# A list scheduler that reckons with longer transposing DMAs: the same work in another static order

## The chip, the cores and the metric

The kernel runs on one core of one Trainium2 chip. The metric is the device time of one execution in microseconds (us), lower is better; the time before is the median of three executions. The core has a matrix engine (PE, with its weight loads shown apart as PEld), a vector engine (DVE), a scalar engine (ACT), a general engine (POOL) and a queue engine (SP) that issues DMAs. ACT issues some DMAs too. Each engine runs its own list of instructions strictly in the order in which it stands, and semaphores make it wait for the others.

## The reference, cut to what matters

```python
# attention with a threshold: batch 4, heads 8, 576 positions, head size 64
scores = q @ k^T / 8
thresh = max(scores) - tau
scores = where(scores >= thresh, scores, -1e9)
attn   = exp(scores - max) / (sum + 1e-9)
x      = (attn @ v) as 2304 tokens x 512
# dense layer pair, leaky ReLU
h = x @ w_in;  g = max(0.01 * h, h);  x = g @ w_out          # 512 -> 2048 -> 512
# soft mixture of 8 experts, 4 slots each
logits = x @ phi                                              # 2304 x 32
d = softmax of logits over the tokens;  slot_in = d^T @ x
slot_out[e] = relu(slot_in[e] @ w1[e]) @ w2[e]                # 512 -> 1024 -> 512
out = (softmax of logits over the slots) @ slot_out
```

All inputs are float32, and w_in and w_out arrive as 64-bit patterns that the kernel takes apart.

## The kernel before

The 2304 tokens are worked in 18 tiles of 128. For each tile, `attention(t)` makes four pairs of heads. For one pair PE computes the scores of both heads (line 1087, called S here), DVE takes the negated row maximum (line 1100, nm), ACT the exponential (line 1121, ae), DVE the masked product and the row sum (line 1128), ACT rounds the result to half precision (line 1154, the high half of ah) and POOL subtracts to get the low half (line 1164). A transposing DMA on SP then turns each head's ah, nine blocks of 128x128, into aT (line 1186, two a pair, 144 in all), and PE multiplies aT with the values into the tile X (line 1196, called X here, 14 matmuls for a head). After eight heads DVE scales X into x32, PE transposes it (line 1229), and ACT and DVE write it as xT.

`feed(t)` multiplies xT with w_in in four column groups of 12 matmuls (line 1267, called H here, dealt out in portions of three), ACT and POOL or DVE make the two halves of r (lines 1280, 1286, 1289), a transposing DMA of eight blocks makes rT (line 1312, 72 in all), and PE multiplies rT with a product of w_out and phi into the logits of the tile (lines 1322 and 1326, called L here). `block` adds every two tiles to the running softmax over tokens. The last part, the tail, starts when the logits of tile 17 are there: it loads w1 and w2 through loads of 256 KB each on SP (line 1691, 128 of them, besides 16 loads of line 1627) into whatever buffers the main part has given free, multiplies (lines 1660, 1703, 1771) and stores the output.

No order is written by hand. Every piece of work is handed to `Plan.add` with a duration and a priority, and `Plan.schedule` is a list scheduler: it keeps a model of each engine's free time, of buffers and of the DMA engines, picks again and again the piece that can start first (the priority breaks ties), and appends it to that engine's list. Where a piece has alternatives (DVE or POOL, SP's queue or ACT's), it also picks the engine. The result is the static order in which the program is emitted; the durations act at planning time alone. A transposing DMA goes through `dma_t`: its `ns` is the time for which the model's DMA engines are held; SP itself is held by `op.hold`, whose first number is a formula in the blocks and whose second, 1300 ns, is the time from issue to the first transfer. The table `LAT` adds 942 ns between the end of a DMA and the PE instruction that reads its data. So the plan before lets PE read an aT 1300 + 9 x 112 + 942 = 3250 ns after its issue if the DMA engines are free.

Of the kernel before, what the change touches and what calls it, by code (L numbers as in the profile page):

```python
# [341 lines left out]
def emit(tc, a, out, dbg=None, opt=None):  # L342
    nc = tc.nc
    pe, act, dve, pool, sp = nc.tensor, nc.scalar, nc.vector, nc.gpsimd, nc.sync
    ctx = ExitStack()
    pl = Plan()
# [37 lines left out]
    one = lambda e, ns, f: [(e, ns, f)]  # L384
# [13 lines left out]
    def const(shape, dt=F32):  # L398
        uniq[0] += 1
        n = f"c{uniq[0]}"  # L400
        pl.tag(n, "const", 1)
        return pl.buf(n, shape, dt)
# [43 lines left out]

    def dma_t(prio, blocks, fn, r=(), w=(), after=()):

        op = pl.add(prio, one("sp", 112.0 * blocks, fn), r, w, after)
        op.hold = (max(1225.0, 398.0 + 112.0 * blocks), 1300.0)  # L450
        return op

    def dump(name, b, sel, prio=1e9):
# [13 lines left out]
        r=[ident], w=[e4],  # L467
# [4 lines left out]
        r=[e4], w=[e96],  # L472
# [9 lines left out]
        r=[tau], w=[sg],  # L482
# [6 lines left out]
        r=[tau], w=[nt],  # L489
# [235 lines left out]
    for k in range(4):  # L725
# [19 lines left out]
        r=[zf], w=[zfr],  # L745
# [17 lines left out]
    for c in range(FF // P):  # L763
        PQ = PO + O["PS"] * c
        here = c < O["RES"]
        w = one_chunk(
            PQ, a["w_out"], c * P, 0, (O["TO"], O["TU"], "raw_out"),
            dst=const([P, DM]) if here else None,
        )
# [5 lines left out]
                r=[w],  # L775
# [5 lines left out]
        def f(w=w, tp=tp):  # L781
# [11 lines left out]
            r=[tp], w=[wt],  # L793
# [3 lines left out]
        def f(wt=wt, wpp=wpp):  # L797
# [7 lines left out]
            r=[wpp], w=[(wp32, c)],  # L805
# [7 lines left out]
        r=[wp32], w=[pm],  # L813
# [8 lines left out]
        r=[spw], w=[wp32],  # L822
# [9 lines left out]
        r=[wp32, (wq, 0)], w=[(wq, 1)],  # L832
    )
    wlq = const([P, 4, 2 * NS], F16) if O["TR"] < O["TE"] else None
    if wlq:
# [3 lines left out]
        for k in range(4):  # L839
            wts = []  # L840
            for j in range(4):
                wt = tmp([P, 8, P], F16, O["TL"])
                dma_t(
                    PL + 0.01 * k, 8,
                    (lambda k, j, wt: lambda: sp.dma_start_transpose(
                        out=wt.ap, in_=wh[k][j].ap.rearrange("p a b -> p (a b)")))(k, j, wt),
                    r=[wh[k][j], wq], w=[wt],
                )
                wts.append(wt)
            lp = tmp([P, 2 * NS], F32, "misc")  # L850

            def f(wts=wts, lp=lp):
# [16 lines left out]
                r=[lp], w=[(wl32, k)],  # L869
# [7 lines left out]
            w=[wl32],  # L877
# [9 lines left out]
            r=[wl32, (wlq, 0)], w=[(wlq, 1)],  # L887
# [247 lines left out]
    def attention(t):  # L1135
# [5 lines left out]
        for pr in range(4):  # L1141
# [40 lines left out]
            for i in range(2):  # L1182
                aT = pl.buf("aT", [P, 9, P], F16)
                dma_t(
                    p2, 9,
                    (lambda ah, aT, i: lambda: sp.dma_start_transpose(out=aT.ap, in_=ah.ap[:, i]))(ah, aT, i),
                    r=[(ah, (n, i)) for n in range(3)], w=[aT],
                )

                todo = [(c, wv, 4 * i + c) for wv in range(2) for c in range(4)]  # L1190
                todo += [(4, wv, 8 + i) for wv in range(2)] + [(5 + c, 0, 4 * i + c) for c in range(4)]

                def f(pr=pr, i=i, aT=aT, todo=todo):
                    for r0, r1, b in regs:
                        for n, (c, wv, cv) in enumerate(todo):
                            pe.matmul(  # L1196
                                out=X.ap[r0:r1, 2 * pr + i], lhsT=aT.ap[:, c, r0:r1],
                                rhs=vtiles[b, pr].ap[:, wv, cv], start=(pr == 0 and i == 0 and n == 0),
                                stop=(n == len(todo) - 1), skip_group_check=True,
                            )  # L1200

                pe_op(
                    p + 0.22, 29 * 14 * len(regs), f, r=[aT] + [vtiles[b, pr] for b in parts], w=[X],
                )
# [48 lines left out]
    def feed(t, xT, xh):  # L1253
# [4 lines left out]
        for j in range(4):  # L1258
# [37 lines left out]
            else:  # L1296
# [11 lines left out]
                    r=[hp, (r[j], 0)], w=[(r[j], 1)],  # L1308
                )
            dma_t(  # L1310
                p + 0.1, 8,
                (lambda j: lambda: sp.dma_start_transpose(
# [308 lines left out]
    for c in range(FF // P):  # L1621
        if wos[c]:
# [5 lines left out]
            w=[wo], after=[stores[c]], la=2 if c < O["NA"] else 0,  # L1628
# [58 lines left out]
    def load(src, prio, shape=(P, 512)):  # L1687
        w = pl.buf(CH, shape, F32, "ch")
        nld[0] += 1
        la = 2 if 16 + nld[0] <= O["NA"] else 0  # L1690
        lds.append(dma(prio, t_dma(P * 512 * 4), lambda dq: dq.dma_start(out=w.ap, in_=src), w=[w], la=la))
        return w

    for G in range(2):
        for n in range(2):
            h1 = pl.buf("S", [P, 512])
            for k in range(4):
                for j in range(4):
                    e = 4 * G + j
                    w = load(a["w1"][e, k * P : (k + 1) * P, n * 512 : (n + 1) * 512], T0 - 7)  # L1700
# [6 lines left out]
                        r=[sit, w], w=[(h1, j)],  # L1707
# [26 lines left out]
    for t0 in range(0, NTILE, 4):  # L1734
        m = min(4, NTILE - t0)
        e3, cp = tbuf([P, m, 3, NS]), pl.buf("misc", [96, m, P])
        if t0 % 8 == 0:
# [4 lines left out]
            r=[(ecs, t) for t in range(t0, t0 + m)], w=[e3])  # L1742

        def f(m=m, e3=e3, cp=cp):
# [8 lines left out]
            op=ALU.subtract))(cp, ct, o4, m), r=[cp], w=[(ct, o4)])  # L1753
# [5 lines left out]
    for hf in range(2):  # L1759
        pt = T0 + 2 + hf  # L1760
        for G in range(2):
            for c in range(0, 8, 2):
                for j in range(4):
                    q = hts[G]
                    w = load(
                        a["w2"][hf, 4 * G + j, c // 2].rearrange("p (k d) -> p k d", k=2), T0 - 7, [P, 2, HC]
                    )
# [26 lines left out]
        for t in range(0, NTILE, 2):  # L1794
            op, ot = pl.buf(("h", "S", "misc")[t // 2 % 3], [P, 2, HC]), pl.buf(CH, [P, 2, HC], F32, "ot")
# [7 lines left out]
            for i in range(2):  # L1803
# [10 lines left out]
                    r=[op, rc], w=[(ot, i)],  # L1814
# [5 lines left out]
                r=[ot], la=2,  # L1820
# [57 lines left out]
```

## Time and profile before

| what | value |
|---|---|
| median of 3 executions | 628.68 us (627.34 to 630.64) |
| the profiled execution, own time | 625.68 us |
| its span, first to last instruction | 623.9 us |
| mean granted clock of PE | 0.969 |
| busy in the span: PE, DVE, ACT, POOL | 509.2, 438.0, 425.3, 342.9 us |

The span has three parts: about 80 us in which inputs are loaded and w_in is taken apart, about 440 us in which the 18 tiles go through, and the rest, in which the last tile's feed ends and the tail runs. The profiled execution is 3.0 us quicker than the median. "Busy" is the time in which an engine had an instruction running; who waited for whom is inferred from semaphores.

### The profile page before, as it was taken

Reading aid. Unit: us, or ns where it says so; the run is one execution under the profiler, and the core shown is the slowest. Engines: PE = TensorE matmul, PEld = TensorE weight load, DVE = VectorE, ACT = ScalarE, POOL = GpSimd, SP = SyncE. Lnnn points to the kernel's source line nnn. Section 1 sums busy time; section 2 is a strip of 40 time slices with the busy share of each in tenths; the row PEclk is TensorE's granted clock in tenths of the full one; section 3 lists DMA queues with packets and bytes.
Section 4 is the critical chain, followed back from the end, with each engine's and each line's share of the span. In section 5 each row is a group of like instructions: output and inputs, shape, how many; then the busy total and the mean of one; then the engine's idle time right before and its main releaser. Section 6 shows DMA issues by size and latency. Waiting matters only on the chain.

```text
span 623.9 us, 15356 instructions
## 1 busy us (share of the span) xinstructions
PE 509.2 (82%) x5694; PEld 318.3 (51%) x5694; DVE 438.0 (70%) x1055; ACT 425.3 (68%) x802; POOL 342.9 (55%) x381
## 2 busy tenths in 40 slices
PE   0111698998899998898999899998999798479995
PEld 0001586666566665555555556565656454223653
DVE  6999978889779777878879777765878743211133
ACT  7999778987668777878978787777777752212012
POOL 3445444775667565787877767777787650000000
PEclk9999998999999999999999999999999989779997
DMA  8972799998899998999999999999998999999998
GB/s 315 328 270 63 209 229 210 236 231 181 177 226 195 220 194 142 197 158 205 228 191 149 173 166 167 212 203 199 183 174 155 212 190 268 288 392 386 379 394 316
DMA packets 287018, 140.55 MB, mean 225 GB/s; under 512 B 251616, under 2 KB 251616, under 8 KB 286944
## 3 DMA queue, kind: packets, MB, share of 16 engines
q1 hardware_dynamic: 281472, 129.05, 91.2%
q10 hardware_dynamic: 5472, 10.52, 6.4%
q8 instruction: 45, 0.74, 0.5%
q14 instruction: 29, 0.24, 0.1%
HBM read 69.27 MB, written 8.91 MB: 125 GB/s over the span
## 4 chain that ended last, share of the span: by engine, by line
PE 42%; DMA 17%; DVE 15%; ACT 11%; POOL 6%; issue 6%; SPq 1%; ACTq 0%; POOLq 0%; DVEq 0%
PE h L1267 14%; DMA aT<-ah 12%; PE S L1087 7%; PE X L1196 6%; PE X L1771 4%; POOL ah L1164 4%; DVE nm L1100 3%; DVE ae L1128 3%; PE S L1703 3%; DMA rT<-r 2%; PE misc L1495 2%; ACT ae L1121 1%; ACT ah L1154 1%; DVE w L640 1%; DMA rT<-in_w_out 1%
## 5 line engine op out<-in xcount | busy, mean ns | idle before, releaser
L1164 POOL TENSOR_TENSOR ah<-ae,ah 128x512 f16<-128x512 f32 (+1 forms) x216 | 203.1, 963 | 92.4 <-ACT ah L1154 71.9
L1267 PE MATMUL h<-wh,xT 128*128 128x512 f16 x864 | 213.8, 384 | 3.5 <-ACT xT L1233 1.7
L1100 DVE TENSOR_REDUCE nm<-S 128x1 f32<-128x576 f32 x144 | 103.6, 750 | 47.0 <-PE S L1087 46.7
L1121 ACT ACTIVATE ae<-S,nm 128x576 f32<-128x576 f32 x144 | 101.5, 735 | 42.6 <-DVE nm L1100 34.6
L1128 DVE SCALAR_TENSOR_TENSOR ae<-S,th,ae 128x576 f32<-128x576 f32 x144 | 114.0, 814 | 9.4 <-ACT ae L1121 8.3
L1267 PEld LDWEIGHTS <-xT 128*128 128x128 f16 x864 | 76.2, 99 | 79.8 <-issue 7.0
L1196 PE MATMUL X<-vx,aT 128*128 128x64 f16 (+1 forms) x2240 | 90.3, 197 | 19.1 <-DMA aT<-ah 18.0
L1196 PEld LDWEIGHTS <-aT 128*128 128x128 f16 (+1 forms) x2240 | 78.6, 103 | 49.8 <-DMA aT<-ah 31.2
L1154 ACT ACTIVATE ah<-ae 128x576 f16<-128x576 f32 x144 | 95.3, 680 | 9.6 <-DVE ae L1128 8.8
L1087 PE MATMUL S<-kx,qh 64*128 64x288 f32 (+1 forms) x620 | 79.8, 328 | 5.2 <-DVE ae L1128 4.9
L1289 POOL TENSOR_TENSOR r<-g,r 128x512 f16<-128x512 f32 x49 | 56.8, 1159 | 19.4 <-ACT r L1286 19.3
L1087 PEld LDWEIGHTS S<-kx,qh 64*128 64x128 f32 (+1 forms) x620 | 54.0, 189 | 24.5 <-issue 16.6
L1280 ACT ACTIVATE g<-h 128x512 f32<-128x512 f32 x72 | 42.7, 593 | 28.7 <-PE h L1267 27.9
L1087 PE MATMUL S<-kx,ql 64*128 64x288 f32 (+1 forms) x300 | 49.3, 303 | 11.2 <-DVE ql L975 11.2
L1286 ACT ACTIVATE r<-g 128x512 f16<-128x512 f32 x72 | 45.1, 629 | 1.0
L1087 PEld LDWEIGHTS S<-kx,ql 64*128 64x128 f32 (+1 forms) x300 | 32.5, 190 | 11.6 <-DVE ql L975 11.6
L496 PE MATMUL misc<-c,tmp 128*1 128x128 f32 x16 | 4.3, 364 | 34.3 <-DVE tmp L563 29.8
L1289 DVE TENSOR_TENSOR r<-g,r 128x512 f16<-128x512 f32 x23 | 20.2, 878 | 13.5 <-ACT r L1286 11.6
L1113 POOL TENSOR_SCALAR th<-nm,c 128x1 f32<-128x1 f32 x49 | 14.8, 302 | 22.9 <-DVE nm L1100 14.7
L1322 PE MATMUL misc<-c,rT 128*128 128x64 f16 x288 | 19.1, 191 | 6.7 <-DMA rT<-r 6.5
L1322 PEld LDWEIGHTS <-rT 128*128 128x128 f16 x288 | 17.6, 97 | 9.3 <-DMA rT<-r 7.1
L799 PEld LDWEIGHTS misc<-c,w 128*128 128x128 f32 x128 | 19.5, 226 | 5.3 <-DVE w L791 2.0
(312 smaller groups left out, 805.5 us busy)
## 6 DMA issues: line engine op xcount, KB each, us to landing
wh<-in_w SPq DMA_DIRECT2D x27, 256.0 KB, 5.4
r<-in_w SPq DMA_DIRECT2D x25, 256.0 KB, 5.1
rT<-in_w_out SPq DMA_DIRECT2D x23, 256.0 KB, 3.7
ah<-in_w_in SPq DMA_DIRECT2D x9, 512.0 KB, 5.9
kx<-in_w SPq DMA_DIRECT2D x15, 256.0 KB, 5.3
ae<-in_w_in SPq DMA_DIRECT2D x7, 512.0 KB, 5.1
scr<-w SPq DMA_DIRECT2D x14, 256.0 KB, 4.0
vr<-in_v SPq DMA_DIRECT2D x11, 320.0 KB, 4.1
```

The lines of the kernel that those rows point to most:

```text
L1087: pe.matmul(out=pss[i].ap[:rows, n, :HALF], lhsT=l.ap[64 * i : 64 * i + 64, pr, :rows], rhs=m.ap[64 * i : 64 * i + 64, n * HALF : (n + 1) ...
L1100: lambda: dve.tensor_reduce(out=nm.ap, in_=ps.ap[:, :, :HALF], axis=AX.XY, op=ALU.max, negate=True),
L1121: lambda: act.activation(out=e(), in_=ps.ap[:, :, :HALF], func=AF.Exp, bias=nm.ap[:, 0:1], scale=1.0),
L1128: lambda: dve.scalar_tensor_tensor(out=e(), in0=ps.ap[:, :, :HALF], scalar=th.ap[:, 0:1], in1=e(), op0=ALU.is_ge, op1=ALU.mult, accum_out= ...
L1154: (lambda ah, ae, i: lambda: act.activation(out=ah.ap[:, i, :S], in_=ae.ap[:, i], func=AF.Copy))(ah, ae, i),
L1164: (lambda ah, ae: lambda: pool.tensor_tensor(out=ah.ap[:, h, w0 : w0 + c1 - c0], in0=ae.ap[:, h, c0:c1], in1=ah.ap[:, h, c0:c1], op=ALU.su ...
L1196: pe.matmul(out=X.ap[r0:r1, 2 * pr + i], lhsT=aT.ap[:, c, r0:r1], rhs=vtiles[b, pr].ap[:, wv, cv], start=(pr == 0 and i == 0 and n == 0), ...
L1267: pe.matmul(out=hp.ap, lhsT=xT.ap[:, wx * 4 + k], rhs=wh[k][j].ap[:, ww], start=(n == 0), stop=(n == 11),)
L1280: (lambda g, hp: lambda: act.activation(out=g.ap, in_=hp.ap, func=AF.Prelu, alpha=0.01))(g, hp),
L1286: (lambda j, g: lambda: act.activation(out=r[j].ap[:, 0], in_=g.ap, func=AF.Copy))(j, g),
L1289: fg = lambda eng, j, g: lambda: eng.tensor_tensor(out=r[j].ap[:, 1], in0=g.ap, in1=r[j].ap[:, 0], op=ALU.subtract)
L1322: pe.matmul(out=L.ap, lhsT=rT[j].ap[:, c], rhs=wq.ap[:, 4 * j + c], start=(j == 0 and c == 0), stop=False,)
```

## The change

In `dma_t` the duration of a transposing DMA goes from 112 to 172 ns a block: 1008 to 1548 ns for an aT, 896 to 1376 ns for an rT. `op.hold` is left as it was.

```diff
     def dma_t(prio, blocks, fn, r=(), w=(), after=()):
 
-        op = pl.add(prio, one("sp", 112.0 * blocks, fn), r, w, after)
+        op = pl.add(prio, one("sp", 172.0 * blocks, fn), r, w, after)
         op.hold = (max(1225.0, 398.0 + 112.0 * blocks), 1300.0)
         return op
```

The same 3319 pieces of work are emitted. The first 358 stand in the same order; from there on, at about the first aT, the lists of all engines differ. Some choices of engine differ too: of the small threshold operations (lines 1107 and 1113) 32 go from POOL to DVE and 15 the other way, of the subtractions for r (line 1289) 12 go from POOL to DVE and 8 the other way, and ACT issues 61 DMAs instead of 38, SP accordingly fewer.

PE, in tile 8 at its third pair of heads, before: the rows of line 1087 are the last four matmuls of that pair's S, and right behind them stands the first X of the tile (aT and vx are its factors; a name's number tells one buffer from another).

```order
L1087 MATMUL S_4593<-kx_2470,qh_3856 128x288
L1087 MATMUL S_4594<-kx_2470,qh_3856 128x288
L1087 MATMUL S_4593<-kx_2460,ql_3891 128x288
L1087 MATMUL S_4594<-kx_2460,ql_3891 128x288
L1196 LDWEIGHTS aT_4532
L1196 MATMUL X_4618<-vx_1051,aT_4532 128x64
```

The same place on PE now: behind the same S stand H portions of an earlier tile (xT and wh are their factors).

```order
L1087 MATMUL S_4447<-kx_2375,qh_3650 128x288
L1087 MATMUL S_4448<-kx_2375,qh_3650 128x288
L1087 MATMUL S_4447<-kx_2350,ql_3693 128x288
L1087 MATMUL S_4448<-kx_2350,ql_3693 128x288
L1267 LDWEIGHTS xT_3964
L1267 MATMUL h_4379<-wh_454,xT_3964 128x512
```

Twelve H matmuls (four portions) have moved in between this S and the first X of the tile, which stands behind them.

PE, at the end of the main part, before: the transposes of tile 17's x (line 1229) are followed by tile 17's H, whose first portion begins here; the logits of tile 16 come after six of its sixteen portions.

```order
L1267 LDWEIGHTS xT_8706
L1267 MATMUL h_8994<-wh_535,xT_8706 128x512
L1229 MATMUL h_9097<-c1_78,x32_9091 128x128 x4
L1267 LDWEIGHTS xT_9108
L1267 MATMUL h_9116<-wh_220,xT_9108 128x512
```

The same place on PE now: the logits of tile 16 (lines 1322 and 1326, which read rT) stand straight behind the transposes.

```order
L1495 LDWEIGHTS dh_9059
L1495 MATMUL misc_9066<-r_8698,dh_9059 32x512
L1229 MATMUL h_9095<-c1_78,x32_9064 128x128 x4
L1322 LDWEIGHTS rT_8919
L1322 MATMUL misc_9110<-c76_2476,rT_8919 128x64
L1326 LDWEIGHTS rT_8919
L1326 MATMUL misc_9110<-c76_2476,rT_8919 128x32
```

L of tile 16 has moved ahead of all sixteen H portions of tile 17, and the update of the running sum (line 1495) to just ahead of the transposes.

SP, at its last rT transposes, which are those of tile 17, between loads of the tail (from in_w1 into buffers named wh, r and so on), before:

```order
L1312 DMA_TRANSPOSE rT_9191<-r_9144 128x8x128
L1691 DMA wh_9216<-in_w1 128x512
L1691 DMA wh_9221<-in_w1 128x512
L1312 DMA_TRANSPOSE rT_9223<-r_9210 128x8x128
L1691 DMA wh_9240<-in_w1 128x512
L1312 DMA_TRANSPOSE rT_9245<-r_9234 128x8x128
L1691 DMA r_9251<-in_w1 128x512
L1691 DMA r_9254<-in_w1 128x512
L1312 DMA_TRANSPOSE rT_9256<-r_9249 128x8x128
L1691 DMA r_9258<-in_w1 128x512
```

The same place on SP now:

```order
L1691 DMA wh_9192<-in_w1 128x512
L1312 DMA_TRANSPOSE rT_9201<-r_9184 128x8x128
L1312 DMA_TRANSPOSE rT_9223<-r_9208 128x8x128
L1691 DMA wh_9234<-in_w1 128x512
L1312 DMA_TRANSPOSE rT_9239<-r_9228 128x8x128
L1691 DMA r_9245<-in_w1 128x512
L1691 DMA r_9248<-in_w1 128x512
L1312 DMA_TRANSPOSE rT_9250<-r_9243 128x8x128
L1691 DMA r_9252<-in_w1 128x512
```

Behind the last rT there are 101 loads of the tail in the order before and 104 now: three have moved behind it.

## Rows read from the trace of the kernel before

**Rows 1.** The page: busy time by engine; the chain's shares by engine.

```profile
PE 509.2 (82%) x5694; PEld 318.3 (51%) x5694; DVE 438.0 (70%) x1055; ACT 425.3 (68%) x802; POOL 342.9 (55%) x381
PE 42%; DMA 17%; DVE 15%; ACT 11%; POOL 6%; issue 6%; SPq 1%; ACTq 0%; POOLq 0%; DVEq 0%
```

**Rows 2.** Busy by engine, first stretch of 40 us and sum, 80 to 520 us.

```profile
core 0: us, PE busy (x) PEld busy (x) DVE busy (x) ACT busy (x) POOL busy (x), PEclk, DMA share, GB/s
80.00:120.00 40.00, 36.37 (x353) 28.81 (x352) 32.88 (x88) 32.99 (x71) 23.57 (x26) 0.96 1.00 230
...
sum 440.00, PE 406.24 PEld 262.76 DVE 343.31 ACT 334.88 POOL 307.18; mean PE 36.93 PEld 23.89 DVE 31.21 ACT 30.44 POOL 27.93
```

**Rows 3.** PE's waits, 80 to 520 us: us in total, times, longest us.

```profile
PE X L1196 <- DMA aT<-ah: 18.0, 24, 1.9
PE S L1087 <- DVE ae L1128: 4.9, 14, 0.7
...
PE h L1267 <- ACT xT L1233: 1.7, 3, 0.9
```

**Rows 4.** The aT transposes, whole span: issue ns min/median/max, a waiter, landing.

```profile
L1186 SPq DMA_TRANSPOSE aT<-ah x144: 1241/1327/3109, 70.5 to 512.9; - x144
...
PEld L1196: 31.2, 40
...
DMA to landing us min/median/max: 3.2/3.9/7.1
```

**Rows 5.** SP's queue, 302 to 321 us: start, us, line, transpose.

```profile
302.38 7.68 SPq L1186 DMA_TRANSPOSE aT<-ah  x4
310.16 2.63 SPq L1312 DMA_TRANSPOSE rT<-r  x2
312.95 3.36 SPq L1186 DMA_TRANSPOSE aT<-ah  x2
316.37 1.35 SPq L1312 DMA_TRANSPOSE rT<-r  x1
317.88 2.81 SPq L1186 DMA_TRANSPOSE aT<-ah  x2
```

**Rows 6.** The chain in order of time: start us, us, what.

```profile
255.76 2.59 PE h L1267 x12
258.35 0.99 PE S L1087 x12
...
405.49 0.97 PE X L1196 x28
...
520.63 5.96 DMA rT<-r
...
527.02 6.50 PE h L1267 x30
...
535.59 4.11 DMA rT<-r
```

**Rows 7.** PE's timeline: end of one pair's S, and its two X.

```profile
306.42 0.38 PE L1087 MATMUL S<-kx,ql 64*128 64x288 f32 x2
...
317.00 0.57 PE L1196 MATMUL X<-vx,aT 128*128 128x64 f16 x14
318.38 0.58 PE L1196 MATMUL X<-vx,aT 128*128 128x64 f16 x14 [0.16 <-DMA aT<-ah]
```

**Rows 8.** A load issued by ACT's queue, from its timeline.

```profile
341.87 0.33 ACTq L966 DMA_DIRECT2D qr<-in_q  x1
```

**Rows 9.** PE's timeline at 517 us, the last H of tile 16.

```profile
517.34 0.81 PE L1267 MATMUL h<-wh,xT 128*128 128x512 f16 x3
```

**Rows 10.** SP's timeline at 518 to 520 us, loads of the tail.

```profile
518.07 0.56 SPq L1691 DMA_DIRECT2D vx<-in_w  x1
...
520.10 0.43 SPq L1691 DMA_DIRECT2D xT<-in_w  x1
```

**Rows 11.** Stretches of the tail, columns as in rows 2.

```profile
580.00:590.00 10.00, 9.99 (x109) 6.78 (x103) 0.80 (x8) 0.00 (x0) 0.00 (x0) 1.00 1.03 373
590.00:600.00 10.00, 9.47 (x46) 4.62 (x47) 3.90 (x9) 1.47 (x4) 0.00 (x0) 1.00 1.05 397
```

## Prediction

> **What bounds the kernel now.** I read the page's busy line and chain first, then the table of 40 us stretches, then who PE waits for, then the transposing DMAs one by one, and last the end of the main part. PE is the busiest engine and has the largest part of the chain, DMA the second [rows 1]. Between 80 and 520 us PE is busy 406.24 of 440 us, so at most 33.8 us can be won there by order alone; DVE, ACT and POOL have 97, 105 and 133 us to spare in the same stretch [rows 2]. Of PE's idle time one kind is large: X waiting for the landing of its aT, 18.0 us in 24 waits, the longest 1.9 us; next come S waiting for DVE (4.9 us) and H waiting for xT (1.7 us) [rows 3]. The same wait seen from the weight loads, which start ahead of the matmuls, is 31.2 us in 40 waits [rows 4]; only the 18.0 us are time in which PE stood. So the main part is bound by PE's work plus a wait that comes from where X stands in PE's list.
>
> **How long a transpose takes, against the planner's number.** The plan before lets PE read an aT 3.25 us after its issue on a free queue, the plan now 1300 + 1548 + 942 = 3.79 us. The trace has 3.2 us at the least, 3.9 in the median and 7.1 at the most [rows 4]. In a train of eleven transposes, 8 aT and 3 rT, 96 blocks, SP needs from 302.38 to 320.69 us, 18.3 us or 191 ns a block [rows 5]; that bounds the rate from above only, since some of it is SP waiting for POOL. The old number is the quickest case, the new one is close to the median. The Trainium skill, page "DMA: Bandwidth & Descriptors", section "Latency and other measured facts", speaks against the change: it gives a DMA transpose some 350 to 400 GB/s when contiguous and 261 GB/s in a measured worse case. An estimate from it for the 294,912 bytes of an aT is 0.74 to 1.13 us, 82 to 126 ns a block, about the old 112. The trace does not agree for the time until the data can be used, 3.9 us in the median, nor for the train's 191 ns.
>
> **The change, part by part.**
>
> First, where X stands. I took PE's list in both orders, gave each piece its duration from the rows (12 S matmuls 0.99 us, a portion of three H 2.59 / 4 = 0.65 us, an X of 14 matmuls 0.97 / 2 = 0.49 us [rows 6]) and added what lies between the end of a pair's S and the start of its two X. Mean before: 10.8 us to the first X, 12.2 us to the second. Mean now: 12.5 and 14.3 us. Against that stands the way through DVE, ACT, POOL and the DMA. One example: the S ends at 306.80 us, the second aT of the pair is what its X waits for at 318.38 us, so 11.5 us [rows 7]. Over the 72 pairs, from the one whose S ends at 62.6 us to the one whose S ends at 505.2 us, the median from S to the landing is 10.8 us for the first head and 12.7 us for the second. In the order before 71 of the 144 X have less PE work behind their S than that median, in the order now 29. That alone says which way the waits go. For a size I set each place against all 72 measured ways and took the mean shortfall: summed over tiles 2 to 17 it falls to 0.47 of its value. The sum itself counts a delay several times, since one wait also covers for the X that follow, so I use the ratio alone: of the 18.0 us about 8.5 stay, **9.5 us are won**. Both ends: all 18.0 us, if a pair's way gets no longer; and a loss of 2.6 us, if the long ways belong to places (the rival below). I take the ratio, since neither the ways nor the places are all alike in the trace.
>
> Second, xT. The PE work between a tile's transposes and its first H grows from 1.6 to 4.6 us in the mean, so the 1.7 us of H waiting for xT [rows 3] may go. The PE work from one S to the next is unchanged (4.45 and 4.43 us), and an engine that is quicker by 2% reaches S earlier by about 0.1 us where S already waits for DVE, 14 places, 1.4 us. I set the two off against each other: 0, between -1.7 and +1.4.
>
> Third, buffers. X later means an aT is held longer, and there are three. Of the 141 places at which an aT has to wait for the X three before it, 7 instead of 3 have less than 4.5 us of PE work for a DMA of 3.9 us. Four more places at perhaps 0.5 us each: 0 to 2 us, I take 0.5.
>
> Fourth, engines. 23 DMAs go from SP's to ACT's queue, at 0.33 us each [rows 8] 7.6 us of ACT's queue over 440 us in which ACT has 105 us to spare [rows 2]. ACT's queue runs ahead of its engine, so most of it is covered; if a load has to wait for its buffer there, the ACT work behind it waits too, and with it the ah of a pair. I take 0, and up to 3 us for the range. The few operations that change between POOL and DVE are a few us on engines with about 100 us spare: 0.
>
> Fifth, the end of the main part. In the order before, the last portion of tile 16's H ends at about 518.0 us, the transposes of x follow [rows 9], the last rT of tile 16 is issued at 520.63 us and takes 5.96 us, longer than the median because five loads of the tail were issued just ahead of it, from 518.07 to 520.10 us [rows 10], and after L of tile 16 ten H portions remain, 6.50 us from 527.02 us [rows 6]. So the last H ends 15.5 us after tile 16's. Now two X and the update of the running sum (1.4 us) stand behind that last portion of tile 16 instead of ahead of it, so it comes 2.4 us earlier; its rT has no load ahead of it. With 2.6 us up to the issue, 3.9 us landing, 0.8 us for the wait's end and L, and sixteen portions at 0.65 us, 10.4 us, the last H ends 17.7 - 2.4 = 15.3 us after the same point; with a landing of 5.96 us 17.4. So -0.2 to +1.9 us, I take 0.
>
> Sixth, the loads of the tail. From the last rT on they run one behind another at 373 to 397 GB/s [rows 11], and the program ends a fixed time after the last. Three more stand behind the last rT, 3 x 262,144 bytes at about 385 GB/s: **+2.0 us**. What would hide it is that PE, not the loads, ends the tail; PE is busy 9.5 to 10 of 10 us there [rows 11], so 0 to 2.0, and I take 2.0.
>
> The sum: -9.5 + 0 + 0.5 + 0 + 0 + 2.0 = **-7.0 us**. Against the profiled execution's own 625.68 us that is 618.7 us; the median of the runs is 3.0 us higher, so the forecast for the median is 628.7 - 7.0 = **621.7 us**.
>
> **The rivals.**
>
> All the waits go: the ways get no longer, every X finds its aT. Then -18.0 - 1.7 + 2.0 = -17.7, 611.0 us. For it: no wait is longer than 1.9 us [rows 3], and the mean distance grows by 1.7 and 2.0 us. Against it: 29 places stay short, among them the last tiles', which have the same distance in both orders.
>
> No change: the gain is real on PE but the pace is set elsewhere, S and H wait for ACT, DVE or POOL in place of X, and what is left, say 2 us, goes on the loads: 628.7, give or take 2. For it: DVE is busy 78% of the stretch and the chain has 32% on DVE, ACT and POOL [rows 1, 2]. Against it: none of the three has a stretch in which it is full. The page's rule above leads to the same time: if a transpose were over after about 1.1 us, the aT would not be what X waits for, and moving X would win nothing; the trace has X waiting for the DMA itself [rows 3].
>
> Slower: the long ways belong to places, not to the order. At four pairs the X come with less PE work behind their S than before, though the mean grows: at the second pair of tiles 2, 6 and 10 and the third of tile 10, 0.3 to 4.6 us less. If each of the 144 ways stayed as it was measured at its place, PE's aT waits would come out at 21.6 us against 19.0 us by the same count: +2.6 us. With the loads' 2.0 us and 1.9 us for L of tile 16 that is +6.5, **635.2 us**. It decides as soon as less than about 4 us of the aT waits go. For it: at the second pair of tiles 2 and 6 the measured ways are 13.2 to 15.2 us, far above the medians. Against it: the plan moved the work of the other engines there as well.
>
> **How the numbers follow.** The partial gain 0.50 (621.7), all waits gone 0.14 (611), no change 0.17 (628.7), slower 0.19 (635.2). The first two are faster by over 0.5%, which is 3.1 us and about what a measurement of this kernel can tell from no change: 0.64; the third is within it, the fourth beyond it. The likeliest case has its own range from 616 to 626 with the bounds of ACT's queue, the buffers and the end of the main part. To hold 8 in 10 the range goes from 611 up into the slower case, to 634.
>
> **What would show it.** In the profile of the changed kernel: the wait of X for aT below 11 us in place of 18.0; PE busy the same 406 us in a stretch that is shorter by some 9 us; the landing of an aT still 3.9 us in the median, since its transfer is not changed; S waiting for DVE under 7 us; the last rT's issue some 9 us earlier than 535.59 us [rows 6] and the end 90 instead of 88 us behind it. Wrong would be an aT wait that stays at 18 us or more (places, not distance), a new wait of ACT or SP on a load's buffer, or a tail that starts earlier and ends no earlier.

## The result and the profile after

The changed kernel takes 622.48 us (median of 20 executions, 616.59 to 629.21), the one before 630.83 us (20 executions, 623.96 to 637.1, measured with it). The ratio is 0.988, its 95% interval 0.985 to 0.990: **8.4 us or 1.2% faster**; forecast were 7.0 us. Single executions of one kernel lie over 12 us apart, so the profile of before, at 625.68 us, is a quick one of its kernel. Rows of after are from an execution of 619.5 us with a span of 617.7 us; the first profile of after (627.85 us) and those of three experiments (639.45 us in the first half of the change, 636.64 us in the other half, 657.62 us with the new choices alone) are of disturbed executions, so their waits and ways count for less than the timed ratios.

The page's busy line, in answer to [rows 1], and then the table of stretches, in answer to [rows 2]:

```profile
PE 512.9 (83%) x5694; PEld 326.0 (53%) x5694; DVE 447.1 (72%) x1071; ACT 424.6 (69%) x803; POOL 342.3 (55%) x364
```

```profile
80.00:120.00 40.00, 36.90 (x314) 29.82 (x314) 32.30 (x81) 33.19 (x72) 21.76 (x22) 0.83 0.95 221
...
sum 440.00, PE 416.50 PEld 273.83 DVE 354.77 ACT 336.58 POOL 306.50; mean PE 37.86 PEld 24.89 DVE 32.25 ACT 30.60 POOL 27.86
```

Between 80 and 520 us PE now stands 23.5 us where it stood 33.8. But it also takes 3.7 us more over the whole span for the same 5694 matmuls; in the first stretch the granted clock is 0.83 in place of 0.96 (last section). Who PE waits for, 80 to 520 us, in answer to [rows 3]:

```profile
PE X L1196 <- DMA aT<-ah: 7.8, 11, 1.7
PE h L783 <- DVE w L664: 5.2, 4, 2.2
PE misc L1433 <- ACT E L1410: 2.8, 2, 1.6
PE X L1196 <- DVE x L1218: 1.7, 2, 0.9
```

The wait of X for aT goes from 18.0 to 7.8 us. The waits of S for DVE and of H for xT are no longer among the first; the preparing of the weights (line 783) waits 5.2 us where it waited 1.7, line 1433 2.8 us where it waited 0.2, and X for DVE 1.7 us where it waited 0.8. Taken together these others change nothing: PE stands 10.3 us less, and the wait for aT alone is 10.2 us less. What the aT transposes themselves did, in answer to [rows 4]:

```profile
L1186 SPq DMA_TRANSPOSE aT<-ah x144: 1241/1316/3994, 70.6 to 504.4; - x144
...
  PEld L1196: 12.8, 14
  PE X L1196: 7.8, 11
...
DMA to landing us min/median/max: 3.2/4.1/7.5
```

The transfer is not faster (4.1 against 3.9 us); PE comes later. What it costs is in the waits of SP's own queue, of before and then of after (a transpose waits for the X that still reads its buffer):

```profile
SPq L1186 <- PE X L1196: 2.6, 3, 1.6
```

```profile
SPq L1186 <- PE X L1196: 29.7, 29, 4.2
```

The end of the main part, from the chain of after, in answer to [rows 6]:

```profile
514.02 10.38 PE h L1267 x48
...
527.40 5.37 DMA rT<-r
```

The last rT is issued at 527.40 instead of 535.59 us, 8.2 us earlier, and the span ends 617.7 - 527.4 = 90.3 us behind it instead of 623.9 - 535.59 = 88.3 us, 2.0 us more, as the sum had it for the three loads. By stages: the last pair's S starts 9.0 us earlier (495.2 for 504.2 us), from there to the last rT it takes 0.8 us more, from there to the end 2.0 us more, which leaves 6.2 us.

### The profile page after: what moved, and what is told of

Its sections match the earlier page's. It is cut to its first block, busy times and chain, and to the rows that moved or that the text cites. A ratio compares the mean times of both kernels' runs of the same rounds, so it can differ in the third digit from the quotient of the medians.

```text
span 626.0 us, 15337 instructions
## 1 busy us (share of the span) xinstructions
PE 512.1 (82%) x5694; PEld 325.5 (52%) x5694; DVE 446.1 (71%) x1071; ACT 424.7 (68%) x803; POOL 341.6 (55%) x364
## 3 DMA queue, kind: packets, MB, share of 16 engines
q10 hardware_dynamic: 8784, 16.81, 10.2%
## 4 chain that ended last, share of the span: by engine, by line
PE 59%; DMA 14%; DVE 10%; ACT 9%; issue 3%; POOL 3%; SPq 1%; ACTq 0%; DVEq 0%; POOLq 0%
PE h L1267 24%; PE S L1087 9%; PE X L1196 8%; DMA aT<-ah 7%; PE X L1771 5%; PE S L1703 2%; POOL ah L1164 2%; DVE nm L1100 2%; DMA wh<-in_w 2%; DVE w L640 2%; PE misc L799 2%; PE misc L1495 1%; DMA vr<-in_v 1%; PE misc L1322 1%; DMA r<-in_w 1%
## 5 line engine op out<-in xcount | busy, mean ns | idle before, releaser
L1128 DVE SCALAR_TENSOR_TENSOR ae<-S,th,ae 128x576 f32<-128x576 f32 x144 | 114.1, 813 | 13.8 <-ACT ae L1121 12.2
L1196 PEld LDWEIGHTS <-aT 128*128 128x128 f16 (+1 forms) x2240 | 82.6, 104 | 41.0 <-DMA aT<-ah 17.6
L1196 PE MATMUL X<-vx,aT 128*128 128x64 f16 (+1 forms) x2240 | 91.4, 198 | 13.6 <-DMA aT<-ah 12.5
L1087 PE MATMUL S<-kx,qh 64*128 64x288 f32 (+1 forms) x600 | 77.3, 332 | 0.6 <-DVE c L938 0.4
L1289 POOL TENSOR_TENSOR r<-g,r 128x512 f16<-128x512 f32 x45 | 53.2, 1185 | 16.5 <-ACT r L1286 16.5
L1087 PEld LDWEIGHTS S<-kx,qh 64*128 64x128 f32 (+1 forms) x600 | 52.2, 193 | 18.7 <-issue 16.0
L1087 PE MATMUL S<-kx,ql 64*128 64x288 f32 (+1 forms) x280 | 46.1, 310 | 11.2 <-DVE ql L975 11.2
L1087 PEld LDWEIGHTS S<-kx,ql 64*128 64x128 f32 (+1 forms) x280 | 29.9, 195 | 11.6 <-DVE ql L975 11.6
L1289 DVE TENSOR_TENSOR r<-g,r 128x512 f16<-128x512 f32 x27 | 23.9, 887 | 16.4 <-ACT r L1286 14.8
L799 PE MATMUL misc<-c,w 128*128 128x32 f32 x128 | 22.8, 332 | 2.4 <-DVE w L791 1.6
L799 PEld LDWEIGHTS misc<-c,w 128*128 128x128 f32 x128 | 22.2, 258 | 4.5 <-DVE w L791 2.0
L1322 PEld LDWEIGHTS <-rT 128*128 128x128 f16 x288 | 17.8, 99 | 11.6 <-DMA rT<-r 9.7
```

The source lines that it names most:

```text
L799: pe.matmul(out=wpp.ap, lhsT=wt.ap[:, k], rhs=phi.ap[:, k], start=(k == 0), stop=(k == 3))
L1087: pe.matmul(out=pss[i].ap[:rows, n, :HALF], lhsT=l.ap[64 * i : 64 * i + 64, pr, :rows], rhs=m.ap[64 * i : 64 * i + 64, n * HALF : (n + 1) ...
L1128: lambda: dve.scalar_tensor_tensor(out=e(), in0=ps.ap[:, :, :HALF], scalar=th.ap[:, 0:1], in1=e(), op0=ALU.is_ge, op1=ALU.mult, accum_out= ...
L1196: pe.matmul(out=X.ap[r0:r1, 2 * pr + i], lhsT=aT.ap[:, c, r0:r1], rhs=vtiles[b, pr].ap[:, wv, cv], start=(pr == 0 and i == 0 and n == 0), ...
L1289: fg = lambda eng, j, g: lambda: eng.tensor_tensor(out=r[j].ap[:, 1], in0=g.ap, in1=r[j].ap[:, 0], op=ALU.subtract)
L1322: pe.matmul(out=L.ap, lhsT=rT[j].ap[:, c], rhs=wq.ap[:, 4 * j + c], start=(j == 0 and c == 0), stop=False,)
```

## The experiments

**The theory**: PE's list puts more work between S and X, the aT has landed by then, and the time that X waited is won. **Rivals**: that only the planned landing matters or only the planned occupation of the DMA engines; that the different choices of engine and queue bring the gain; that the three aT buffers end it when X moves further; that the gain is not in the aT wait at all; that the change is only one more order of many, lucky by chance. Ratios are to the kernel before on the same chip, with 95% intervals. Waits of PE are over 80 to 560 us. "Distance" is PE's work between the end of a pair's S and its first X; "way" is the measured time from the same point to the landing of the first aT (means over the tiles, as in the prediction; way over tiles 2 to 17). Before: distance 10.8, way 10.8 us. Changed: 12.5 and 11.6. The distance is counted from the list with a mean duration for each kind of piece, so a few tenths between the two are not to be relied on.

**The changed kernel once more**, to have its spread and a second profile.

> The changed kernel once more, for a profile that is not disturbed. Theory (X stands farther behind S, so PE waits less for aT): about 1.2% under the kernel before (ratio 0.985 to 0.990), PE's wait of X for aT 8 to 12 us against 18.0, in a span some 7 to 9 us shorter. Rival (the gain is in the choice of engines and queues, not in X's place): the same ratio, but the wait of X for aT within 2 us of 18, and the gain in other waits.

Measured: 621.77 us, 0.989 (0.983 to 0.995). The rows above are its profile.

**The order before without its aT wait.** X multiplies a constant tile of the same shape in place of aT; the transposes still run, but nothing waits for them and their buffers come free at once.

```diff
-   out=X.ap[r0:r1, 2 * pr + i], lhsT=aT.ap[:, c, r0:r1],
+   out=X.ap[r0:r1, 2 * pr + i], lhsT=ident.ap.bitcast(F16)[:, r0:r1],
```

> The order before, but X multiplies a constant tile instead of aT, so no X waits for a transposing DMA; the 144 transposes are still issued. The kernel thus leaves the attention product out; every engine's order is word for word that of before. It prices all the aT waits of the order before. Theory: 15 to 20 us under the kernel before (ratio 0.968 to 0.976), since the 18.0 us are on the path. Rival (PE's idle time moves to the next wait): 0 to 6 us (ratio 0.99 to 1.0).

Measured: 622.56 us against 630.35 us for the kernel before on this chip, 0.988 (0.983 to 0.992). **The 18.0 us were worth 7.8 us**, between what the theory and the rival had forecast. Its waits of PE, and its timeline at 522 us:

```profile
PE misc L1322 <- DMA rT<-r: 15.6, 7, 4.1
PE S L1087 <- DVE ae L1128: 6.3, 15, 1.1
```

```profile
522.11 0.23 PE L1322 MATMUL misc<-c,rT 128*128 128x64 f16 x1 [4.11 <-DMA rT<-r]
```

In the kernel before, the first of these rows reads:

```profile
PE misc L1322 <- DMA rT<-r: 6.5, 3, 3.3
```

PE reaches L earlier by what it no longer waits at X, and stands there for rT: 9.1 us more. The last pair's S starts 9.2 us earlier than in the profile of before (495.0 us), the last L ends only 2.1 us earlier (538.1 us). The 2.1 us are not the whole worth, for PE was also slower at its work in this execution: 512.2 us busy at a mean clock of 0.947, against 509.2 us at 0.969. Its idle time, shown for all six kernels further down, fell by 6.8 us, near the 7.8 us timed.

**The changed order without its aT wait**, the same edit in the changed kernel.

> The same constant tile in the changed order. Theory: the two orders differ by the aT waits and three loads behind the last transpose, so without the waits they come within 3 us of each other, this one 0 to 3 us slower (ratio to the kernel before 0.968 to 0.981). Rival (the other moves of the change make the gain): this one stays 6 to 9 us under the order before without aT waits.

Measured: 615.74 us, 0.979 (0.974 to 0.984). So 6.8 us lie between the two orders although no X waits for an aT in either. That does not fit the theory as I had put it; it is what the rival had forecast. The wait of L for rT, in this run and in the changed kernel as it is:

```profile
PE misc L1322 <- DMA rT<-r: 7.6, 4, 3.8
```

```profile
PE misc L1322 <- DMA rT<-r: 7.3, 4, 3.4
```

Here the wait does not come back at L. This pointed to the other transposing DMA, whose planned time the same line of the change lengthens.

**Both orders without the waits for aT and for rT**: L too multiplies the constant tile.

```diff
-   out=L.ap, lhsT=rT[j].ap[:, c], rhs=wq.ap[:, 4 * j + c],
+   out=L.ap, lhsT=ident.ap.bitcast(F16)[:, 0:P], rhs=wq.ap[:, 4 * j + c],
```

(The same edit stands in the second matmul of L, line 1326; it is left out here.)

> The order before; X and L multiply a constant tile instead of aT and rT, so that PE waits for no transposing DMA at all; all 216 transposes are still issued. The attention product and the logits are thus left out. Without the aT waits alone this order came to a ratio of 0.988, and 6.3 us of new waits of L for rT stood in its trace. Theory A (the change's gain is the distance of PE's work to the transposing DMAs, X and L alike): both orders without both waits come together, this one at 0.977 to 0.983 and within 0.4% of the changed order without both. Theory B (the gain is in other waits, S for DVE and H for xT, 6.2 and 3.8 us in the trace without aT waits): this one stays at 0.983 to 0.990, and 0.8 to 1.2% above the changed order without both.

> The changed order with the same constant tile for X and L. Without the aT waits alone it came to 0.979. Theory A and B: 0.974 to 0.980, as its rT waits before the end are 0.4 us and only those of tiles 16 and 17 remain (some 7 us in all, at the end of the main part). What tells A from B is the difference from the order before without both waits: under 0.4% for A, 0.8% or more for B.

Measured: order before 615.79 us, 0.982 (0.977 to 0.987); changed order 613.54 us, 0.980 (0.976 to 0.985). **The two orders come together**: 2.3 us apart and the intervals overlap nearly whole, where 8.6 us lay between the kernels as they are and 6.8 without the aT wait. Thus most of the gain is in what PE waits for at the two transposing DMAs taken together; the 2.3 us that are left cannot be told from nothing. PE's idle time, which leaves out how fast PE itself worked, says the same. From 80 us to the end of the last L, PE's columns (the stretch, its length, PE's busy time and matmuls, clock, DMA share, GB/s) of the two kernels as they are (before, then changed), of the two without the aT wait, and of the two without both:

```profile
80.00:540.24 460.24, 419.56 (x5052) 0.98 1.03 197
80.00:533.32 453.32, 422.54 (x5052) 0.96 1.04 199
80.00:538.11 458.11, 424.20 (x5050) 0.95 1.04 198
80.00:528.80 448.80, 420.22 (x5054) 0.97 1.08 201
80.00:514.10 434.10, 412.53 (x5050) 0.98 1.07 202
80.00:517.70 437.70, 417.38 (x5050) 0.96 1.05 201
```

PE stands 40.7 and 30.8 us, then 33.9 and 28.6, then 21.6 and 20.3 us: the gap between the orders shrinks from 9.9 to 5.3 to 1.3 us. What limits each then, PE's largest wait, order before and changed order:

```profile
PE S L1087 <- DVE ae L1128: 8.0, 21, 0.8
```

```profile
PE h L783 <- DVE w L664: 4.9, 3, 2.2
```

**Half of the change: DMA engines held for 172 ns a block, landing planned as with 112.**

```diff
-   o.end = s + ns
+   o.end = s + ns + o.late
     def dma_t(...):                  # shortened; 172.0 * blocks stands in pl.add
+        op.late = -60.0 * blocks     # 0 for all other pieces
```

> One half of the change: the planner holds its DMA engines 172 ns a block for a transpose, but reckons its data as landed after 112 ns a block. In PE's list the mean work between S and X is 12.7 and 14.4 us (12.5 and 14.2 in the changed order, 10.8 and 12.2 before). Theory (distance): the ratio of the changed kernel within 0.4%, 0.982 to 0.992. Rival (the later landing is what the order needs): no gain, 0.995 to 1.005.

Measured: 633.93 us, 1.005 (1.001 to 1.008). Distance 12.7 us, longer than in the changed kernel, and no gain, as the rival had it: the ways grew nearly as much, to 12.5 us. I had expected the whole gain. Line numbers are 2 higher here; its waits of X, and of SP for X:

```profile
PE X L1198 <- DMA aT<-ah: 16.0, 15, 3.6
```

```profile
SPq L1188 <- PE X L1198: 24.6, 23, 3.4
```

SP waits for buffers nearly as in the changed kernel, without what that bought there. Six loads of the tail more than before stand behind the last rT (107, not 101), which by the prediction's 0.68 us a load is 4.1 us; in the changed kernel it is three.

**The other half: landing planned with 172, engines held for 112**, by `op.late = 60.0 * blocks` with 112.0 in `pl.add`.

> The other half of the change: the planner's DMA engines are held 112 ns a block as before, but the data is reckoned as landed 60 ns a block later. Mean work between S and X 11.5 and 12.9 us, 58 short places, 42 DMAs on ACT's queue (38 before, 61 changed). Theory A, with the other half at 1.005 although its distance was the longest: what counts is the distance less the way, and here the plan's way is right and the queue is not thinned; 0.988 to 0.996, aT waits 11 to 16 us. Rival (only both halves together give anything): 0.997 to 1.005.

Measured: 629.41 us, 0.997 (0.993 to 1.001): less than expected, not to be told from nothing, and in the range of the rival (only both halves together). Distance 11.5, way 11.5 us, and X waits as before (numbers 2 higher):

```profile
PE X L1198 <- DMA aT<-ah: 21.1, 28, 2.2
```

**Which part do the engine choices have?** Two kernels with a list of choices pinned: the plan with 172 ns and the choices of the kernel before, and the plan with 112 ns and those of the changed one. The lists are read off the two plans (shortened):

```diff
+   many = [o for o in ops if len(o.alts) > 1]
+   for o, c in zip(many, CHOSEN, strict=True):
+       o.alts = [x for x in o.alts if x[0] == NAME[c]]
```

> The planner reckons with 172 ns a block as in the change, but every choice of engine or queue (DVE or POOL, SP's queue or ACT's) is pinned to what the plan before chose. The mean work between S and X is 11.7 and 13.2 us (10.8 and 12.2 before, 12.5 and 14.2 in the changed order), 42 short places (82 before, 39 changed). Theory A (order makes the gain): 0.985 to 0.994. Rival C (the 23 DMAs that went to ACT's queue and the moves between POOL and DVE make it): no gain, 0.996 to 1.004.

> The reverse: planned with 112 ns a block, every choice of engine or queue pinned to that of the changed kernel. Mean work between S and X 10.9 and 12.4 us, 84 short places, as before. Theory A: no gain, 0.996 to 1.004. Rival C: most of the gain, 0.986 to 0.992.

Measured: long DMA with old choices 621.57 us, 0.992 (0.988 to 0.995); short DMA with new choices 651.36 us, 1.036 (1.030 to 1.042). The waits of X for aT, in that order (numbers 15 higher):

```profile
PE X L1211 <- DMA aT<-ah: 11.5, 11, 2.9
```

```profile
PE X L1211 <- DMA aT<-ah: 33.1, 28, 4.3
```

The longer DMA time alone keeps most of the gain (distance 11.7, way 11.1 us); what is missing, 0.4%, is within the intervals. The new choices in a plan that does not reckon with longer transposes harm: distance 10.9, way 11.3 us. By themselves the choices do not bring the gain.

**Other values in the same line: 142 and 202 ns a block.**

> Planned with 142 ns, half the step. Mean work between S and X 11.2 and 12.7 us, 70 short places, L 17.7 us behind H, 101 loads behind the last rT. Theory A: half the gain at most, 0.992 to 0.999, aT waits 14 to 18 us. Rival (the change is one more order of many, and its luck does not follow the number): anywhere from 0.98 to 1.02, aT waits not between those of before and changed.

> Planned with 202 ns a block instead of 172. The mean work on PE between S and X is 18.4 and 20.5 us, 10 short places (39 in the changed order, 82 before), L stands 38.7 us of PE work behind the last H of its tile in the mean (24.8 and 13.9), and 110 loads stand behind the last rT (104 and 101). Theory A (PE's list must stand far enough behind the transposing DMAs): X waits for aT under 3 us; the main part as in the orders without these waits, 0.978 to 0.982, and 9 loads of 0.68 us more behind the last rT: 0.985 to 0.992. Rival D (a longer lag fills the three aT buffers and the r buffers, and SP and ACT wait for those): slower than the changed kernel, 0.993 to 1.010, with SP waiting for X by 10 us or more.

Measured: 142 ns 631.55 us, 1.002 (0.998 to 1.005), distance 11.2 and way 11.4 us; 202 ns 654.84 us, **1.039 (1.035 to 1.044)**, distance 18.4 and way 18.3 us. With 142 X still waits, 19.5 us where 14 to 18 were expected, more than in the kernel before: no gain and a wait outside 7.8 to 18.0 us are what the rival of luck had forecast, and the times do not follow the number (1.000, 1.002, 0.988, 1.039 for 112, 142, 172, 202). With 202 X hardly waits, and SP does. The waits of X with 142 and with 202, and those of SP's queue with 202:

```profile
PE X L1196 <- DMA aT<-ah: 19.5, 22, 1.7
```

```profile
PE X L1196 <- DMA aT<-ah: 2.4, 2, 1.9
```

```profile
SPq L1186 <- PE X L1196: 104.1, 71, 3.7
SPq L1186 <- POOL ah L1164: 78.9, 66, 4.8
```

71 times a transpose waits for a buffer there, for 144 transposes, 104.1 us against 29.7 and 2.6. The aT wait is gone, and yet 32 us more than in the changed kernel: the last pair's S starts 12 us later (507.3 us), from there to the last L it takes 55 us instead of 38, since so much work was put off, and the rest 91 instead of 84, with 110 loads behind the last rT instead of 104. PE's waits have moved, and its work takes longer. Two of its waits with 202, and its busy time (512.9 us in the changed kernel):

```profile
PE S L1087 <- DVE ae L1128: 10.3, 16, 1.7
PE h L1267 <- ACT g L1280: 5.7, 6, 2.2
```

```profile
PE 529.0 (81%) x5694; PEld 335.1 (51%) x5694; DVE 455.4 (70%) x1084; ACT 421.1 (64%) x796; POOL 329.4 (50%) x358
```

The mean clock is 0.940 in place of 0.956. So of the 35.4 us between the two spans (653.1 and 617.7 us) 16.1 us are PE's longer time for the same matmuls, and the rest is time in which PE stands. Whether SP's waits bring on both was not tried by itself. The forecast of the rival, 0.993 to 1.010, was far too low as well.

**The kernel before, one more profile**, at 621.65 us:

> The kernel before once more, for a second profile: the first one ran 5 us under the median of its runs. All theories: the same waits as in the first profile, X for aT 16 to 20 us of 80 to 520 us; if the first was quick because PE ran less at the lower of its two clock levels, this one shows more of that between 90 and 120 us.

```profile
PE X L1196 <- DMA aT<-ah: 14.0, 20, 1.9
```

That is less than the 16 to 20 us expected. This execution is quicker still than the first one profiled, and its clock is much the same (0.72 and 0.94 at 95 to 100 and 100 to 105 us, there 0.68 and 0.98), so it doesn't tell why the first was quick. The aT wait of one and the same kernel is 18.0 in one execution and 14.0 in another; in the other execution of after it was 12.5, not 7.8. Readings of a few us in such a row are no more than that, and of the runs above only those with a timed ratio carry a verdict.

## Why the prediction was right, and where not

**X for aT, -9.5 us.** The wait fell by 10.2 us, to 7.8 where 8.5 were forecast. This size rested on comparing each place with the measured ways, and in these two executions that held; with 14.0 to 18.0 us before and 7.8 to 12.5 us after, one pair of profiles does not fix it. The premise that a us of this wait is a us of the program did not: all 18.0 us, taken away in the order before, bring 7.8, because L then stands for rT. The prediction looked at what X waits for and, but for tile 16 at the end of the main part, left out the second reader of a transposing DMA. Its rival "all the waits go", 611 us, was priced in the same wrong way.

**What made the size come out.** The same number lengthens the planned rT as well: L stands 24.8 us of PE work behind the last H of its tile instead of 13.9, and in the changed order the wait at L stays at 7.3 us. With both waits taken away the orders are alike to within 2.3 us, so most of the 8.4 us is there. That the term of 9.5 lay near it is partly luck: a term for L was missing, and it would have said that the aT term alone gives less.

**The ways.** I took the ways as the same in both orders. They grew by 0.8 us for the first head and 0.9 for the second (11.6 and 13.7 us), while the distances grew by 1.7 and 2.0; what seems to count is the difference. In the half change with the longer distance it was 0.2 us, and there was no gain. That longer ways come from SP waiting for buffers fits the rows of 29.7 and 104.1 us, but the ways were not taken apart further.

**xT and S, 0.** Two waits fell away that I had set off against a rise: S for DVE, 4.9 us, and H for xT, 1.7 us, are no longer listed among the larger ones. In their place line 783 waits 3.5 us more, line 1433 2.6 us and X for DVE 0.9 us. So 0 was right as a sum, though not for the reason given: S did not come to wait longer.

**Buffers, 0.5 us.** The term counted PE places, not SP's queue. 29.7 us of waits there are not on the path as such; with 202 ns SP waits 104.1 us, beside a loss of 3.9% that other things share in. The mechanism was named; what it costs in the changed kernel was not taken apart.

**Engines and ACT's queue, 0; end of the main part, 0; loads, +2.0.** The choices by themselves bring no gain, by the pinned kernels. The last sixteen H portions took 10.38 us (10.4 forecast), and from the last S to the last rT it is 32.2 us in place of 31.4, within the -0.2 to +1.9 given. Behind the last rT 2.0 us are added, as forecast. That it is the loads was not tried by itself, but the other orders bear out the trend: with 101 loads behind it (before twice, 142 ns, the new choices alone) the program ends 87.4 to 90.1 us after the last rT, with 105 (long DMA, old choices) 90.7 us, with 110 (202 ns) 94.2 us. One pair of profiles does not make the 2.0 us exact.

**The rivals.** "No change" would have had S and H wait for DVE, ACT or POOL instead; they wait less. With it falls the estimate of about 1.1 us for an aT, from the bandwidth that the Trainium skill, page "DMA: Bandwidth & Descriptors", section "Latency and other measured facts", gives for DMA transposes. It counted the transfer alone, while the landing takes 4.1 us from the issue in the median, and the move won 1.2%. "Slower" needed long ways that stay at their places. Of its two examples, the second pair of tile 2 came to a way of 10.8 us for its first head (13.2 before), while that of tile 6 stayed long, 16.5 us (13.8 before), with about 9 us of PE work before its X. So the mechanism exists, but at too few places: the aT wait fell. Yet slower was near in another way: 202 ns, one step further, is 3.9% slower.

**Not settled.** Why 142 ns and the landing alone give next to nothing, where 172 ns gives 1.2%, was not found: distance minus way is -0.2 and 0.0 us there and +0.9 in the changed kernel, which fits the times but doesn't tell why the planner's list comes out so. With 202 ns it is 0.1 us, and X hardly waits, so the mean difference is not the whole rule. That 172 ns is a lucky order among its neighbours is thus not ruled out; that its gain comes from the waits for the two transposing DMAs is what the runs show. More aT buffers together with a larger number was not tried. No run made a version that computes the whole result and is, by its ratio, faster than the changed kernel.

## What to carry to other kernels

Price a wait by taking it away, in both orders if there are two, and look which reader stands next: here 18.0 us of waiting were worth 7.8, and only with the second reader of the same kind of DMA included did the two orders come together. A planner's duration is a choice of order, not a fact: it can win while the distance that it buys exceeds the delay that fuller buffers add, and neighbouring values can lie on either side (142 and 202 ns did), so each is to be measured.

## What had not been expected of the hardware

The clock. In the changed order PE stands 2.16 us for a piece of the weights before 94.81 us, and afterwards the granted clock is at the lower of its two levels, 1.2 GHz, for over 10 us, though PE is busy. One row of PE's timeline, and three stretches with their columns as in [rows 2]:

```profile
94.81 0.66 PE L783 MATMUL h<-c,w 128*128 128x128 f32 x4 [2.16 <-DVE w L664]
```

```profile
95.00:100.00 5.00, 5.00 (x50) 4.53 (x50) 4.47 (x10) 4.08 (x9) 3.00 (x4) 0.62 0.92 220
100.00:105.00 5.00, 5.00 (x32) 4.56 (x31) 4.71 (x10) 4.72 (x11) 2.40 (x3) 0.50 1.02 248
105.00:110.00 5.00, 4.26 (x30) 2.58 (x27) 3.00 (x7) 3.64 (x9) 1.54 (x2) 0.52 1.17 238
```

In the profile of before the clock, at the same time, is back at the upper level after one stretch:

```profile
95.00:100.00 5.00, 3.78 (x33) 3.21 (x33) 3.94 (x9) 5.00 (x12) 2.57 (x3) 0.68 0.92 249
100.00:105.00 5.00, 4.17 (x54) 3.37 (x53) 4.88 (x12) 4.03 (x9) 2.40 (x5) 0.98 0.95 196
```

It is not a matter of the order alone. The order before without its aT wait, word for word the same list, shows this in its own execution:

```profile
100.00:105.00 5.00, 5.00 (x37) 4.76 (x38) 4.93 (x10) 3.98 (x9) 2.36 (x5) 0.50 1.01 202
105.00:110.00 5.00, 5.00 (x38) 3.27 (x36) 3.21 (x7) 3.06 (x7) 2.71 (x4) 0.72 1.12 199
```

And the changed order without its aT wait, after the same 2.16 us, has 0.71 and 0.97 in these two stretches.

The Trainium skill, page "TensorE: Matmul & The Clock Gate", section "HAM oscillation — how this bites in real kernels", tells of a wait for data that lets the clock fall, so that the next work starts at the lower level. The rows here agree in part: the clock falls, but 0.62 over the first stretch, if it is one fall, puts that at 96.2 us: the work behind the wait starts at the upper level and loses it 1.4 us later; and in the profile of before it falls too, where no wait between 84 and 100 us is longer than 0.88 us. Why PE stays there in one execution with 5.00 of 5.00 us busy, and rises in another with 4.17, no run here tells. Over the whole program the same 5694 matmuls take 512.9 us of PE at a mean clock of 0.956 and 509.2 us at 0.969. The order before took 506.3 and 512.2 us in two other executions, the second without its aT wait, so these 3.7 us can't be put down to the change.
